# Transformer block on one core: fillers until a slot's last VectorE sum, a second bank for warming matmuls, LayerNorm 2 ahead of VectorE's exps

## The chip, the cores and the metric

The kernel runs on one core of a Trainium2 chip. The metric is the device time in microseconds (us); lower is better. "ACT" is ScalarE, "DVE" VectorE, "PE" TensorE, "POOL" GpSimd, "SP" SyncE (which issues DMAs).

## The reference

x is 2048 x 640, bf16. The block is attention with 32 heads of 20 channels, then a gated MLP of width 1728, each behind a LayerNorm without weights and each added to its input:

```python
qkv = layernorm(x) @ wqkv                       # 32 heads, Dh = 20
p   = softmax(q @ k.T * 20 ** -0.5)             # 2048 x 2048 per head
h   = x + (p @ v) @ wo
out = h + (gelu(layernorm(h) @ w_gate) * (layernorm(h) @ w_up)) @ w_down
```

The first LayerNorm is LN1 here, the second LN2. The softmax is 32 x 2048 x 2048 = 134 million exps, and they are most of the work outside TensorE.

## The kernel before, in words

**A planner writes the order.** The program first collects operations (`op`: engine, instructions, an estimated duration, a priority, what is read and written, PSUM banks taken and given back). Then `Sched.schedule` plays them through in planned time: whenever an engine is free it takes, of the operations that are ready and whose banks are free, the one with the lowest priority number (and on PE prefers the one that keeps the array's mode). The order so found is what each engine's queue gets; `emit` adds the semaphore waits. So a priority or a planned duration has no instruction of its own, but it can change the order on every engine.

**Attention.** The 2048 queries are cut into seven chunks (512, 512, 256, 256, 256, 128, 128). A chunk is worked off in slots (32 in all, 8 for each large chunk, 4 for each of 256, 2 for each of 128); a slot fills one PSUM bank, bank 6, with 4 heads' outputs side by side for 512 columns. Within a slot PE makes tiles of scores (128 keys x 512 columns; line 942, "S"), two or three PSUM banks at a time; ScalarE makes `exp` of them into the buffers `pts`/`pts2` (18 tiles of 512, in turn); PE sums them times V into bank 6 (`pv_op`, tag "O"). A part of the score tiles ("SD", single tiles) goes to VectorE instead: `d_exp` copies the tile out of PSUM (line 877) and makes the exponential in six passes over 1024 or 2048 columns; the sums of these tiles (tag "OD") follow later, at the latest before the slot is closed. When all sums of a slot are done, `epilogue` copies bank 6 out to `osb` (VectorE, line 1025), which frees the bank for the next slot, transposes it (line 1035) and divides by the row sums into `o_nat`. ScalarE can run ahead of the sums only as far as the 18 buffers reach.

**Background.** PE's and VectorE's spare time goes to the other work, in the banks that attention leaves: 7 and 5, and in slots 8 to 15 (chunk 1, where scores use six banks) bank 7 alone (`BG`). In chunk 0 these are the projections. After a chunk's last slot `post` collects the rest of the block for that chunk: `o_nat` is transposed (by DMA on SP's queue for chunks 1 to 5), multiplied with `wo` (line 659), added to x (line 1081); LN2 takes its statistics on VectorE (`ln_stats`: two `bn_stats` of 320 columns and one `bn_aggr` for a tile of 128 tokens), 1/sqrt in 14 small operations on POOL for two tiles together (`ln_rsqrt`), a reciprocal and `ln_apply` on VectorE, DMA transposes; then gate matmuls (line 1114) and copies (line 1149), gelu on ScalarE over all copies of the chunk together, up matmuls (1114 as well) with products (1160), down matmuls (1171) with the last add (1175), and the output's DMA. The last chunk ("tail") has nothing to hide behind: its `post` starts after the last exp.

**Priorities** (a lower number goes first): scores and their copies 0, sums 1, copies that give a bank back 1.8 (`sc.ev`), VectorE's exp passes, epilogue transposes and the tail 2 (`P_EPI`), LN2's matmuls 2.5 (`P_LNP`), LN2 on VectorE and POOL 2.5 (`P_LND`), other background 3.

**Fillers.** PE's clock is granted by use, so the planner adds matmuls without a result. A *zero matmul* group is four matmuls (128 x 32 weights of zeros, 512 columns) that add 0 to bank 6; this is possible while a slot's sums are open in that bank (`live`). They are added to a sum operation, or stand alone where PE has nothing to do. A *warming matmul* writes into a free background bank, bank 7 alone. Both are put in only where PE's planned use over the last 3.4 us is too low:

```python
199                 if e == "pe" and self.pad is not None and o.tag and o.tag[0] == "O":
...
204                     while u < PAD_MIN * PAD_WIN and o.util < 1.1 and o.dur + 0.215 < room:
205                         o.fns = o.fns + self.pad
...
209                     live = o.i not in self.final
```

`final` holds each slot's last sum of ScalarE's exps, so `live` ends there even when sums of VectorE's exps are still to come.

Of the kernel before, what the change touches and what calls it, by code (L numbers as in the profile page):

```python
# [7 lines left out]
ALU = mybir.AluOpType  # L8
# [38 lines left out]
class Sched:  # L47
# [3 lines left out]
    def __init__(self, nc):  # L51
        self.nc = nc
        self.ops = []
        self.lw = {}
        self.rd = {}
        self.warm = None
        self.pad = None
        self.final = set()
        self.ev = 9
# [34 lines left out]
    def schedule(self):  # L94
# [23 lines left out]
        while done < total:  # L118
# [4 lines left out]
            for e in ENGINES:  # L123
# [51 lines left out]
                if chosen is None:  # L175
                    if e == "pe" and self.warm is not None:
                        while recent and recent[0][0] < t - WARM_WIN:
                            recent.popleft()
                        b = self.warm_bank
                        free7 = (owner[b] is None and free_at[b] <= t + 1e-9  # L180
                                 and all(hasattr(ops[d], "fin") and ops[d].fin + 0.06 <= t for d in self.warm_deps))
                        if sum(x for _, x in recent) < WARM_MIN * WARM_WIN and (free7 or live):
                            o = Op()
                            o.i, o.eng, o.lat = len(ops), "pe", DRAIN["pe"]
                            o.prio, o.sem, o.tag, o.util = (9, 0), None, "warm", 0.213
                            o.acq, o.rel, o.succ, o.dur = [], [], [], 0.215
                            if live and (mode[e] == "col" or not free7):
                                o.fns, o.mode, o.deps = list(self.pad), "col", set()
                            else:
                                o.fns, o.mode = [self.warm], "full"  # L190
                                o.deps = set(self.warm_deps) | ({last[b]} if last[b] is not None else set())
                                last[b] = o.i
                            ops.append(o)
                            chosen = o
                            total += 1
                    if chosen is None:
                        continue
                o = chosen
# [128 lines left out]
PV_QUADS = 2  # L327
D_LAG = 9
PR, PR2 = 12, 6
D_QUADS = (1,) + (2,) * 15 + (2, 2) + (3, 2) * 5 + (2, 2, 2, 2)  # L330
# [6 lines left out]
P_QK, P_PV, P_PRO, P_EPI, P_LN, P_BG = 0, 1, 1.5, 2, 2.5, 3  # L337
P_LND, P_LNP = 2.5, 2.5


def bass_sequential_preLN__mha_block__glu_gated_geglu__prompt_kernel(
# [12 lines left out]
    with ExitStack() as es:  # L354
# [545 lines left out]
        def pv_op(s_, quads, acq, seq, after, key):  # L900
# [4 lines left out]
            for have in quads:  # L905
                for kk in range(nk):
                    for pt, pkey, (_, g, kb, j) in have:
# [5 lines left out]
                        pv_open.add((s_, j))  # L913
                        reads += [pkey, ("v", kt, g // 4)]
            return op("pe", fns, 0.222 * len(quads), P_PV, mode="col", util=0.213 * len(quads), reads=reads, writes=[key] + seq,
                      acq=acq, after=after)

        def unit(u):
# [57 lines left out]
            while pv_wait:  # L976
# [74 lines left out]
        def prefetch(c):  # L1051
            q0, nq = CHUNKS[c]
            nt = nq // 128
            tb = base(c)
            op("sp", I("dma_start", h_sb[:, tb:tb + nt, :], x_hbm[q0:q0 + nq, :].rearrange("(t p) d -> p t d", p=128)), 0.08, P_EPI,
               writes=[("h", tb + tt, hf) for tt in range(nt) for hf in range(2)], sem=f"xr{c}", lat=2.0 + nq * 0.0034,
               after=tuple(e_ops) + tuple(w_readers) if c == 0 else ())

        def post(c, first_banks, banks, tail):
# [61 lines left out]
            def cols(k):  # L1121
                return min(512, (NF - k * fn_) * nq)
# [19 lines left out]
            else:  # L1142

                cp, gl = [], []
                for k in range(nb):
# [4 lines left out]
                                 reads=[kg], writes=hkeys(k), rel=[bg], after=first))  # L1150
                for ks in [list(range(i, min(i + 4, nb))) for i in range(0, nb, 4)]:
                    w = 512 * (ks[-1] - ks[0]) + cols(ks[-1])
                    fv = hv(ks[0], w)
                    gl.append(op("act", I("activation", fv, fv, ACT.Gelu_apprx_tanh), c_act(w) + 0.04, -1, mode="gelu",
                                 reads=sum(map(hkeys, ks), []), writes=sum(map(hkeys, ks), []), after=cp))
                for k in range(nb):
                    w = cols(k)
                    fv = hv(k, w)
                    bu, ku = mms(k, wu, "wu", (sc.lw[hkeys(k)[-1]],))
                    hdone.append(op("dve", lambda eng, bu=bu, fv=fv, w=w: eng.tensor_tensor(fv, fv, bank(bu, w),  # L1160
                                                                                                 ALU.mult),
                                    c_dve(w), p, reads=[ku] + hkeys(k), writes=hkeys(k), rel=[bu]))
# [103 lines left out]
```

## Time and profile before

| | |
|---|---|
| time, median of 3 runs | 920.41 us (920.27 to 920.45) |
| profiled execution | 921.39 us, its span 919.4 us |
| granted TensorE clock, mean | 0.991 |
| busy ACT / PE / DVE / POOL | 881.1 / 839.5 / 796.2 / 45.6 us |
| first exp, last exp end | 32.25, 885.04 us |
| ScalarE's table loads | 16, 20.5 us |
| zero matmuls, warming matmuls | 668, 53 |

The profile is one execution seen by the hardware profiler. "Busy" is the time in which an engine runs instructions; for PE, whose matmuls overlap, it is not its peak. A row of the timeline gives start, length, engine, line, operation, out<-in with shapes, and how many of them were merged; in brackets stands the idle time of the engine before it and who ended it. Most instructions have line 362, that of the helper that makes them, and are told apart by tiles: `pts` or `rege` written by ACT are exps, `qt_all` and `rege` on DVE mostly exp passes (their buffers lie in regions named so), `ps<-pts,v_all`, `ps<-rege,v_all` and `ps<-qt_all,v_all` the sums on PE (`rege` holds six of ScalarE's buffers as well as some of VectorE's), `ps<-kt_all,zer` the zero matmuls, `ps<-kt_all` the warming ones.

### The profile page before, as it was taken

What the parts mean: (1) busy time and instruction counts of PE and PEld (TensorE: products, weight loads), DVE (VectorE), ACT (ScalarE), POOL (GpSimd) and SP (SyncE); (2) the same over time, 40 slices, a digit from 0 to 9 for tenths busy, and PEclk for the clock granted to TensorE, in tenths of its full rate; (3) what the DMA queues carried; (4) which work ended last, traced back from release to release, by engine and by line L of the source; (5) the groups of instructions that cost most, each with busy time, mean ns of one, the idle gap of its engine ahead of it and who ended that gap; (6) DMA issues with size and microseconds to landing.
All of it is one profiled execution on the core that took longest, in us unless ns stands there. A gap on an engine that the chain in (4) does not pass through costs nothing.

```text
span 919.4 us, 23006 instructions
## 1 busy us (share of the span) xinstructions
PE 839.5 (91%) x10099; PEld 356.2 (39%) x10099; DVE 796.2 (87%) x1458; ACT 881.1 (96%) x789; POOL 45.6 (5%) x149
## 2 busy tenths in 40 slices
PE   3999999999888987989898999999999899899998
PEld 2432223222232222223342333344444445566677
DVE  8869899999799986887988998989999998959943
ACT  8999899999999999999999999999999999999981
POOL 5000000000002000000011000000201000000200
PEclk9999999999999999999999999999999999999999
DMA  7311021335501000000121000000010001002000
GB/s 258 92 22 43 13 61 35 91 89 137 217 1 30 1 1 1 1 1 16 43 30 31 2 1 1 4 20 24 23 37 2 16 9 39 2 17 39 10 9 23
DMA packets 39515, 34.35 MB, mean 37 GB/s; under 512 B 19436, under 2 KB 36936, under 8 KB 39416
## 3 DMA queue, kind: packets, MB, share of 16 engines
q1 hardware_dynamic: 39416, 32.89, 12.9%
q8 instruction: 79, 1.29, 0.6%
q14 instruction: 20, 0.16, 0.1%
HBM read 20.12 MB, written 8.09 MB: 31 GB/s over the span
## 4 chain that ended last, share of the span: by engine, by line
ACT 67%; PE 23%; DVE 8%; issue 1%; POOL 1%; DMA 0%; DVEq 0%
ACT pts L362 42%; ACT rege L362 23%; PE ps L942 6%; PE ps L1114 5%; PE ps L362 4%; PE ps L659 4%; DVE qt_all L362 3%; PE ps L1171 3%; DVE qt_all L877 1%; DVE rege L877 1%; ACT L362 1%; DVE rege L1149 1%; PE ps L1035 1%; DMA rege<-o_nat 0%; PE ps L601 0%
## 5 line engine op out<-in xcount | busy, mean ns | idle before, releaser
L362 ACT ACTIVATE pts<-ps 128x1024 bf16<-128x1024 f32 (+1 forms) x470 | 563.4, 1358 | 3.8 <-PE ps L942 2.6
L942 PE MATMUL ps<-qt_all,kt_all 32*128 32x256 bf16 (+2 forms) x3584 | 310.1, 290 | 42.9 <-ACT pts L362 23.2
L362 ACT ACTIVATE rege<-ps 128x1024 bf16<-128x1024 f32 (+1 forms) x233 | 289.8, 1353 | 6.1 <-PE ps L362 3.5
L942 PEld LDWEIGHTS ps<-qt_all,kt_all 32*128 32x128 bf16 x3584 | 102.2, 92 | 272.1 <-ACT pts L362 142.4
L362 DVE TENSOR_TENSOR qt_all<-qt_all 128x2048 f16<-128x2048 f16 (+3 forms) x186 | 175.0, 941 | 2.1
L1114 PE MATMUL ps<-rege,regw 128*128 128x256 bf16 (+2 forms) x980 | 159.5, 291 | 12.4 <-ACT rege L362 3.7
L362 PE MATMUL ps<-pts,v_all 128*21 128x256 bf16 (+2 forms) x2070 | 126.6, 293 | 0.0
L877 DVE TENSOR_SCALAR qt_all<-ps 128x512 int16<-128x512 f32 x128 | 87.5, 684 | 16.8 <-PE ps L942 15.5
L877 DVE TENSOR_SCALAR rege<-ps 128x512 int16<-128x512 f32 x128 | 87.6, 685 | 14.7 <-PE ps L942 13.4
L1114 PEld LDWEIGHTS ps<-rege,regw 128*128 128x128 bf16 x980 | 72.6, 98 | 70.9 <-issue 27.0
L362 PE MATMUL ps<-rege,v_all 128*21 128x256 bf16 (+2 forms) x1214 | 93.6, 298 | 0.2
L659 PE MATMUL ps<-regw 128*128 128x512 bf16 (+1 forms) x360 | 87.5, 352 | 2.6 <-ACT regw L607 1.5
L362 DVE TENSOR_SCALAR qt_all<-qt_all 128x1024 f16<-128x1024 int16 (+2 forms) x153 | 84.5, 560 | 1.7
L1171 PE MATMUL ps<-regw,rege 128*128 128x320 bf16 x448 | 77.8, 301 | 1.1 <-DVE rege L1139 0.5
L362 DVE TENSOR_TENSOR rege<-rege 128x1024 f16<-128x1024 f16 (+1 forms) x90 | 61.4, 682 | 0.8
L362 PE MATMUL ps<-kt_all,zer 128*32 128x512 bf16 x668 | 59.8, 398 | 0.0
L362 PEld LDWEIGHTS ps<-pts,v_all 128*21 128x21 bf16 x2070 | 45.4, 91 | 33.8 <-issue 30.4
L1160 DVE TENSOR_TENSOR rege<-rege,ps 128x512 bf16<-128x512 bf16 (+1 forms) x53 | 35.8, 677 | 22.7 <-PE ps L1114 22.3
L362 DVE TENSOR_SCALAR rege<-rege 128x1024 int16<-128x1024 int16 (+2 forms) x115 | 49.3, 442 | 1.0
L1171 PEld LDWEIGHTS ps<-regw,rege 128*128 128x128 bf16 x448 | 37.5, 97 | 32.4 <-issue 16.0
L659 PEld LDWEIGHTS ps<-regw 128*128 128x128 bf16 x360 | 28.8, 99 | 45.0 <-issue 24.2
L1149 DVE CAST rege<-ps 128x512 bf16<-128x512 f32 (+1 forms) x53 | 35.8, 679 | 4.7 <-PE ps L1114 4.7
(105 smaller groups left out, 583.2 us busy)
## 6 DMA issues: line engine op xcount, KB each, us to landing
rege<-in_A_x_dram SPq DMA_DIRECT2D x6, 640.0 KB, 5.1
q_rows<-regw SPq DMA_DIRECT2D x20, 128.0 KB, 1.7
out_dram<-rege SPq DMA_DIRECT2D x16, 160.0 KB, 1.8
regw<-in_B_w_gate_dram SPq DMA_DIRECT2D x1, 2160.0 KB, 11.5
regw<-in_B_w_up_dram SPq DMA_DIRECT2D x1, 2160.0 KB, 16.5
regw<-in_B_w_down_dram SPq DMA_DIRECT2D x1, 2080.0 KB, 21.6
kt_all<-k_rows SPq DMA_DIRECT2D x12, 160.0 KB
qt_all<-q_rows SPq DMA_DIRECT2D x12, 160.0 KB
```

Of the source, the lines that this page charges most:

```text
L362: return lambda eng: getattr(eng, method)(*args, **kwargs)
L659: yield op("pe", lambda eng, l=l, r=r, k=k: eng.matmul(bank(bk, n), l, r, start=(k == 0), stop=(k == len(steps) - 1)), c_mm(n) + cold, pri ...
L877: d_ops.append(op("dve", lambda eng: eng.tensor_scalar(v[:, 512 * h:512 * h + 512], bank(b), EXP_MUL, -32000.0, ALU.mult, ALU.max), c_dve( ...
L942: return lambda eng: eng.matmul(out()[:, kk * nq:(kk + 1) * nq], kt_all[32 * j:32 * j + 32, g, kt * 128:(kt + 1) * 128], qt_all[32 * j:32 ...
L1035: op("pe", lambda eng, tt=tt: eng.transpose(bank(b2)[:, tt * 128:(tt + 1) * 128], osb[:, s, tt * 128:(tt + 1) * 128], identf[:]), c_mm(128 ...
L1114: op("pe", lambda eng, a=a, f=f, fi=fi: eng.matmul(bank(bk)[:, fi * nq:(fi + 1) * nq], w[:, a, F0[f]:F0[f] + 128], hnT[:, a, 128 * tb:128 ...
L1149: cp.append(op("dve", lambda eng, bg=bg, fv=fv, w=w: eng.tensor_copy(fv, bank(bg, w)), c_dve(w), p, reads=[kg], writes=hkeys(k), rel=[bg], ...
L1160: hdone.append(op("dve", lambda eng, bu=bu, fv=fv, w=w: eng.tensor_tensor(fv, fv, bank(bu, w), ALU.mult), c_dve(w), p, reads=[ku] + hkeys( ...
L1171: op("pe", lambda eng, f=f, o=o, hf=hf, bk=bk: eng.matmul(bank(bk, 320), ha_f[:, o:o + 128], wd[:, f, hf * 320:(hf + 1) * 320], start=(f = ...
```

## The change

Five edits:

1. `left` counts a slot's sum operations, O and OD; `live` stays on until the last of them has been issued. An OD operation may now carry zero matmuls too, unless it is the last; the last O operation still may.
2. A warming matmul goes into the first free bank of the current slot's background banks: 7, then 5; in slots 8 to 15 only 7.
3. `P_LND` goes from 2.5 to 1.9: LN2's statistics, POOL chain, reciprocal and apply come ahead of the exp passes (2) and behind the copies that free a bank (1.8).
4. A single score tile for VectorE is planned at 0.21 us also where PE has been idle for over 0.06 us before it.
5. Gate, gelu, up and down of `post` are put in functions, so that chunks named in `MERGE` could share one gelu; `MERGE` is empty.

```diff
-        self.final = set()
+        self.left = {}
...
-                        b = self.warm_bank
-                        free7 = (owner[b] is None and free_at[b] <= t + 1e-9
-                                 and all(hasattr(ops[d], "fin") and ops[d].fin + 0.06 <= t for d in self.warm_deps))
+                        b = next((b for b in self.spare if owner[b] is None and free_at[b] <= t + 1e-9), None)
+                        free7 = b is not None and all(hasattr(ops[d], "fin") and ops[d].fin + 0.06 <= t for d in self.warm_deps)
...
-                                o.fns, o.mode = [self.warm], "full"
+                                o.fns, o.mode = [self.warm[b]], "full"
...
-                if e == "pe" and self.pad is not None and o.tag and o.tag[0] == "O":
+                if e == "pe" and o.tag and o.tag[0] == "S":
+                    self.spare = self.spares[o.tag[1]]
+                if e == "pe" and self.pad is not None and o.tag and o.tag[0] in ("O", "OD"):
+                    s_ = o.tag[1] if o.tag[0] == "O" else o.tag[1][0]
+                    self.left[s_] -= 1
+                    live = self.left[s_] > 0
...
-                    while u < PAD_MIN * PAD_WIN and o.util < 1.1 and o.dur + 0.215 < room:
+                    while u < PAD_MIN * PAD_WIN and o.util < 1.1 and o.dur + 0.215 < room and (live or o.tag[0] == "O"):
...
-                    live = o.i not in self.final
...
-                    if o.tag and o.tag[0] == "SD" and mode[e] != "row":
+                    if o.tag and o.tag[0] == "SD" and (mode[e] != "row" or t - free[e] > 0.06):
                         o.dur = SD_ALONE
...
+MERGE = ()
...
-P_LND, P_LNP = 2.5, 2.5
+P_LND, P_LNP = 1.9, 2.5
...
+            sc.left[s_] = sc.left.get(s_, 0) + 1
             return op("pe", fns, 0.222 * len(quads), P_PV, mode="col", ...
...
-                    sc.final.add(pv)
...
+                gated.append((cp, gelu, ups, lambda: down(c, first, banks, hkeys, hdone)))
+                if c in MERGE:
+                    return
+                for x in gated:
+                    x[1](sum((y[0] for y in gated), []))
+                for x in gated:
+                    x[2]()
+                    x[3]()
+                gated.clear()
+                return
+            down(c, first, banks, hkeys, hdone)
...
-        sc.warm = I("matmul", PS[:, 512 * 7:512 * 8], kt_all[:, 0, 0:128], kt_all[:, 0, 0:512], start=True, stop=True,
-                    skip_group_check=True)
+        sc.warm = {b: I("matmul", PS[:, 512 * b:512 * (b + 1)], kt_all[:, 0, 0:128], kt_all[:, 0, 0:512], start=True, stop=True,
+                        skip_group_check=True) for b in (7, 5)}
+        sc.spare = (7,)
...
-        sc.warm_bank = 7
+        sc.spares = [BG[x[0][0]] for x in units]
```

More of the change, by code (lines that the diff above doesn't have):

```diff
@@ L1057, in prefetch @@
                after=tuple(e_ops) + tuple(w_readers) if c == 0 else ())
+        gated = []
         def post(c, first_banks, banks, tail):
@@ L1142, in post @@
             else:
-                cp, gl = [], []
+                cp = []
                 for k in range(nb):
@@ L1150, in post @@
                                  reads=[kg], writes=hkeys(k), rel=[bg], after=first))
[L1151 to L1162, printed above, removed]
+                def gelu(after):
+                    for ks in [list(range(i, min(i + 4, nb))) for i in range(0, nb, 4)]:
+                        w = 512 * (ks[-1] - ks[0]) + cols(ks[-1])
+                        fv = hv(ks[0], w)
+                        op("act", I("activation", fv, fv, ACT.Gelu_apprx_tanh), c_act(w) + 0.04, -1, mode="gelu",
+                           reads=sum(map(hkeys, ks), []), writes=sum(map(hkeys, ks), []), after=after)
@@ new lines, in ups @@
+                def ups():
+                    for k in range(nb):
+                        w = cols(k)
+                        fv = hv(k, w)
+                        bu, ku = mms(k, wu, "wu", (sc.lw[hkeys(k)[-1]],))
+                        hdone.append(op("dve", lambda eng, bu=bu, fv=fv, w=w: eng.tensor_tensor(fv, fv, bank(bu, w),
+                                                                                                     ALU.mult),
+                                        c_dve(w), p, reads=[ku] + hkeys(k), writes=hkeys(k), rel=[bu]))
@@ new lines, in post, with down @@
+                gated.append((cp, gelu, ups, lambda: down(c, first, banks, hkeys, hdone)))
[9 more added lines that the diff above has]
+            down(c, first, banks, hkeys, hdone)
+        def down(c, first, banks, hkeys, hdone):
+            p = P_BG
+            q0, nq = CHUNKS[c]
+            nt = nq // 128
+            tb = base(c)
+            hb = 1792 * tb
+            fn_ = 512 // nq
```

## The prediction

> **What bounds the kernel now.** I read the page's busy table first, then three stretches of the span, then the stretches at half clock, then single stages.
>
> ```profile
> span 919.4 us, 23006 instructions
> PE 839.5 (91%) x10099; PEld 356.2 (39%) x10099; DVE 796.2 (87%) x1458; ACT 881.1 (96%) x789; POOL 45.6 (5%) x149
> ...
> 0.00:32.25 32.25, 17.80 (x138) 10.64 (x138) 27.83 (x82) 27.51 (x48) 12.85 (x36) 1.00 0.59 200
> 32.25:885.04 852.79, 790.83 (x9584) 320.35 (x9580) 754.19 (x1344) 842.68 (x728) 32.77 (x113) 0.99 0.12 32
> 885.04:919.40 34.36, 30.88 (x386) 25.16 (x382) 14.16 (x34) 10.91 (x14) 0.00 (x0) 1.00 0.06 21
> ```
>
> The columns after the length are busy PE, PEld, DVE, ACT, POOL, then the granted clock. From the first exp to the last (32.25 to 885.04) ScalarE is busy 842.68 of 852.79 us. The change removes no exp, gelu or table load, so at most the 10.1 us of ScalarE's waits can go there. After the last exp PE is busy 30.88 of 34.36 us: the end is PE's, and work done before 885 shortens it. The profiled execution took 921.39 us, of which 919.4 is the span; the median of the three timed runs is 920.41, so I subtract from 921.39 and take off 0.98 for the median.
>
> Where do ScalarE's waits lie? Mostly in five stretches of 3.41 us at half clock.
>
> ```profile
> 88.21:91.62 3.41, 2.02 (x16) 0.69 (x13) 3.41 (x9) 3.41 (x4) 0.00 (x0) 1.00 0.31 95
> 91.62:95.03 3.41, 3.41 (x23) 0.69 (x20) 3.41 (x8) 0.82 (x2) 0.00 (x0) 0.50 0.12 40
> 293.01:296.42 3.41, 2.17 (x28) 0.83 (x23) 3.29 (x9) 3.41 (x4) 0.00 (x0) 1.00 0.26 53
> 296.42:299.83 3.41, 3.41 (x28) 0.79 (x20) 2.96 (x5) 2.57 (x3) 0.00 (x0) 0.50 0.00 0
> 480.74:484.15 3.41, 2.05 (x27) 0.91 (x31) 3.41 (x10) 3.41 (x4) 2.24 (x9) 1.00 0.00 0
> 484.15:487.57 3.42, 3.42 (x44) 1.11 (x44) 2.34 (x6) 2.83 (x3) 1.95 (x8) 0.50 0.25 52
> ...
> 617.27:620.69 3.42, 3.42 (x36) 1.35 (x35) 2.95 (x4) 2.63 (x3) 0.00 (x0) 0.50 0.00 0
> ...
> 668.47:671.89 3.42, 3.42 (x34) 1.79 (x30) 2.65 (x6) 2.29 (x3) 0.00 (x0) 0.50 0.51 149
> ```
>
> ScalarE idles 2.59, 0.84, 0.59, 0.79 and 1.13 us in the five, 5.9 of the 10.1. The stretch ahead of each of the first three has PE busy 2.02 to 2.17 us of 3.41, against 790.83/852.79 = 93% over the whole phase. So the clock halves after a stretch in which PE is little used, though no stretch is empty.
>
> **The change part by part.** *Zero matmuls until the last VectorE sum.* A slot is one pass over a 512-column sum bank (bank 6). The first half-clock stretch stands at slot 1's end:
>
> ```profile
> 87.32 0.61 PE L362 MATMUL ps<-pts,v_all 128*21 128x512 bf16 x7
> ...
> 89.16 1.30 PE L942 MATMUL ps<-qt_all,kt_all 32*128 32x512 bf16 x6 [0.91 <-ACT pts L362]
> ...
> 91.90 0.61 PE L362 MATMUL ps<-rege,v_all 128*21 128x512 bf16 x4
> 92.56 0.69 DVE L362 COPY osb<-ps 128x512 f32<-128x512 f32 x1
> 94.87 2.36 ACT L362 ACTIVATE rege<-ps 128x1536 bf16<-128x1536 f32 x2 [2.59 <-PE ps L362]
> L362 PE MATMUL ps<-kt_all,zer 128*32 128x512 bf16 x668 | 59.8, 398 | 0.0
> ```
>
> The slot's last sum of ScalarE's exps is issued at 87.32, that of VectorE's exps (rege) at 91.90, and between them PE idles 0.91 us with zero matmuls forbidden. The change allows them there: about two groups of four at 0.40 us each. 2.02 us of use becomes some 2.8, so I count this stretch as saved. Its worth is not 2.59: the late sum holds bank 6 anyway until the copy of 92.56 ends at 93.25. Only PE's own steps from 91.90 to 94.87 are lengthened by the clock, some 1.6 us of them on the path (the sum at 91.90 with 0.61, the next slot's first sums with the rest up to 94.87 after 93.25); at full clock about half of that stays, so I take 0.8 us. Bounds: 0 and 2.59. The zeros hide in PE's idle time; without that cover a group would delay the next score matmuls by up to 0.40.
>
> *Warming matmuls into bank 5 as well.* Outside slots 8 to 15 bank 5 is a background bank. It helps where bank 7 is held and PE idles, as ahead of the third stretch:
>
> ```profile
> 483.79 0.39 PE L942 MATMUL ps<-qt_all,kt_all 32*128 32x256 bf16 x6 [0.81 <-ACT pts L362]
> ```
>
> There bank 7 holds the slot's transposed sums. Two or three warming matmuls fit in 0.81 us if bank 5 is free; I count 0.59 us saved, bounds 0 and 0.59.
>
> *LN2 in front of VectorE's exps* (priority 2.5 to 1.9; exps 2.0, bank-releasing copies stay 1.8). Fifteen of the sixteen token tiles go this way. First chunk 0:
>
> ```profile
> 269.42 0.48 DVE L1081 TENSOR_TENSOR rege<-ps,rege 128x320 bf16<-128x320 f32 x1
> ...
> 281.09 0.20 DVE L362 BATCH_NORM_AGGREGATE mv<-stats 128x2 f32<-128x12 f32 x1
> ...
> 291.50 0.44 DVE L362 TENSOR_SCALAR xn_t<-rege,mu,rs 128x640 bf16<-128x640 bf16 x1
> ...
> 298.80 1.03 PE L1114 MATMUL ps<-rege,regw 128*128 128x512 bf16 x2
> ```
>
> The last residual add ends at 269.9, the last statistics 11.4 us later, behind exps. Moved up, the gates start some 10 to 15 us before 298.80 and fill PE in 293 to 296: that stretch's 0.84 us I count as saved. Then chunk 1, from which on the background work is one queue:
>
> ```profile
> 479.24 0.49 DVE L1081 TENSOR_TENSOR rege<-ps,rege 128x320 bf16<-128x320 f32 x1
> ...
> 481.76 0.20 DVE L362 BATCH_NORM_AGGREGATE mv<-stats 128x2 f32<-128x12 f32 x1
> 482.02 0.32 POOL L362 CAST mv<-mv 128x4 bf16<-128x4 f32 x1 [0.70 <-DVE mv L362]
> ...
> 486.50 0.20 POOL L362 TENSOR_TENSOR sd<-nw,rs 128x2 bf16<-128x2 f32 x1
> 488.84 0.16 DVE L362 RECIPROCAL rs<-sd 128x2 f32<-128x2 bf16 x1
> ...
> 493.60 0.44 DVE L362 TENSOR_SCALAR xn_t<-rege,mu,rs 128x640 bf16<-128x640 bf16 x1
> ...
> 497.92 0.81 PE L1114 MATMUL ps<-rege,regw 128*128 128x512 bf16 x3
> ```
>
> The adds end at 479.73. Two statistics and an aggregate (1.1 us) bring 480.9, POOL's chain of 4.7 us 485.6, reciprocal and two applies 486.7 in place of 494.04. From the last apply to the first gate pass 3.9 us of DMA transposes on SP's queue, which keep their order. So 7.3 us at best; copies that keep their place before LN2 (about two of 0.7 us) leave 5.5 to 6; I take 5.5. What is that worth at the end?
>
> ```profile
> L1114 PE MATMUL ps<-rege,regw 128*128 128x256 bf16 (+1 forms) x201 | 23.0, 256 | 0.7 <-DVE rege L1149 0.5
> ...
> L1171 PE MATMUL ps<-regw,rege 128*128 128x320 bf16 x44 | 7.7, 301 | 0.0
> ...
> L1171 PE MATMUL ps<-regw,rege 128*128 128x320 bf16 x112 | 16.2, 299 | 0.6 <-DVE rege L1139 0.5
> L1114 PE MATMUL ps<-rege,regw 128*128 128x128 bf16 x218 | 12.8, 219 | 0.0
> ```
>
> The upper two rows are the groups of 820 to 885.04, the lower two those after it. Of 112 down matmuls after 885 only 28 belong to the last chunk, of 218 gate and up matmuls 140: 84 x 0.145 + 78 x 0.059 = 16.8 us are left over from chunks 4 and 5. From 820 on the background advances (23.0 + 7.7)/65.04 = 0.47 us of PE work per us. A queue that is 5.5 us ahead leaves 2.6 us less behind; bounds 0 (the lead is eaten by bank waits) and 7.3 x 0.47 = 3.4.
>
> The price: what waits behind LN2 on VectorE are the exps' passes, then their sums on PE, the copy that frees bank 6, the next slot's sums, and through the buffers of P ScalarE. Slot 24 ends right after chunk 3's adds:
>
> ```profile
> 689.45 0.49 DVE L1081 TENSOR_TENSOR rege<-ps,rege 128x320 bf16<-128x320 f32 x1
> 690.60 0.40 PE L362 MATMUL ps<-pts,v_all 128*21 128x256 bf16 x8
> ...
> 693.39 0.68 DVE L362 COPY osb<-ps 128x512 f32<-128x512 f32 x1
> ...
> 694.62 0.50 PE L362 MATMUL ps<-pts,v_all 128*21 128x256 bf16 x9
> ...
> L362 DVE BATCH_NORM_STATS2 stats<-rege 128x6 f32<-128x320 bf16 x56 | 25.1, 474 | 0.5 <-DMA rege<-in_A_x_dram 0.5
> ```
>
> Four statistics and two aggregates (4 x 0.474 + 2 x 0.20 = 2.3 us) now go before that copy. At slot 1 ScalarE stopped at 92.28, 4.35 us after the last ScalarE sum ended (87.93). The same distance here is 695.35, while the next sums would run at 696.9 to 697.4: a stall of up to 2.1 us where there is none. Bounds 0 and 2.1; I take 1.0.
>
> *The rest.* The empty merge list leaves the order of gate, gelu, up and down as it is: 0. The longer planned time of a lone score tile adds no instruction; it can only swap neighbours in the order, and one swap can win or lose a half-clock stretch, plus or minus 0.8. I also expect one new half-clock stretch at 0.8, since chunk 0's background ends earlier and leaves PE emptier before 465.
>
> Sum: -2.6 (end), -0.8 -0.59 -0.84 + 0.8 = -1.4 (clock), +1.0 (stall): -3.0. 921.39 becomes 918.4, the median 917.4.
>
> [...]
>
> **The rivals.** *The stall decides.* LN2's passes make the sums late at the ends of slots inside LN2, the next slot's sums wait for bank 6, ScalarE stops. It decides once a slot's copy comes more than about 4 us after its last ScalarE sum and the background's lead is lost to bank waits. For it: VectorE has no gap before 693.39 and slot 1 shows the whole path. Against it: in the other chunks' LN2 the copies come soon after the sum. One stall gives 922.5, two 924.6.
>
> *The lead is eaten.* Background copies, score tiles and epilogues share banks 5 and 7; if these bound the queue, the end keeps its 16.8 us: -1.4 + 1.0, 920.0.
>
> [...]
>
> *All half-clock stretches go.* 0.8 + 0.84 + 0.59 + 0.79 + 1.13 = 4.15 us and the end's 2.6: 913.7.
>
> **How the numbers follow.** Forecast 917.4, chance 0.40 (own range 914.5 to 918.5); all stretches gone 0.08; lead eaten 0.14; fillers idle 0.08; stall 0.30, which is high because the order is planned anew and nothing in it protects a slot's end. 0.2% is 1.84 us, about what a measurement of this kernel can tell from no change. Faster 0.48, same 0.14 + 0.08 = 0.22, slower 0.30. The range takes in the case without half clocks and one stall: 913.5 to 923.0.
>
> **What would show it.** Right: zero matmuls between a slot's last ScalarE sum and its copy near 90; chunk 1's first gate near 492; fewer than 84 left-over down matmuls after the last exp; fewer half-clock stretches. Wrong: ScalarE waiting for sums (PE ps L362) around LN2; as much left over after the last exp; new half-clock stretches at slot ends.

## The result and the profile after

The changed kernel took 915.69 us (median of six runs, 914.24 to 916.19), the kernel before beside it on the same chip 920.34: ratio 0.9946, 95% interval 0.9934 to 0.9959. Forecast were 917.4 us and 913.5 to 923.0. The profiled execution took 916.19 us.

The page's span and busy row of after, and the table by stage: up to the first exp, to the last exp, and the end. The columns are those explained in the prediction.

```profile
span 914.2 us, 22759 instructions
PE 824.1 (90%) x9952; PEld 351.2 (38%) x10017; DVE 794.1 (87%) x1458; ACT 881.1 (96%) x789; POOL 48.2 (5%) x149
...
0.00:33.29 33.29, 18.62 (x136) 10.80 (x138) 27.94 (x82) 27.47 (x48) 12.87 (x36) 1.00 0.57 193
33.29:881.61 848.32, 777.49 (x9439) 317.39 (x9501) 752.96 (x1345) 842.65 (x727) 35.28 (x113) 1.00 0.12 32
881.61:914.20 32.59, 27.98 (x381) 22.97 (x379) 13.18 (x32) 11.02 (x14) 0.00 (x0) 1.00 0.05 16
```

ScalarE's work between the first and the last exp is unchanged (842.65 against 842.68 us), but the stage is 848.32 us long and not 852.79: its waits went from 10.1 to 5.7 us. The end went from 34.36 to 32.59 us. The head is 1.04 us longer; over the profiles of this study it lies anywhere between 32.3 and 33.8 us, also for kernels with the same fillers, and I count it to no edit. -4.47 - 1.77 + 1.04 = -5.2 us, the difference of the spans.

Where did the waits go? Four stretches of the clock's length and the group of the zero matmuls in after:

```profile
88.21:91.62 3.41, 2.83 (x36) 0.84 (x37) 3.41 (x8) 3.41 (x4) 0.00 (x0) 1.00 0.15 53
91.62:95.03 3.41, 3.36 (x35) 0.97 (x27) 3.38 (x8) 2.31 (x3) 0.00 (x0) 1.00 0.31 92
806.97:810.38 3.41, 2.04 (x69) 1.31 (x66) 2.41 (x3) 3.41 (x4) 0.00 (x0) 1.00 0.24 48
810.38:813.80 3.42, 3.42 (x63) 1.82 (x51) 0.00 (x0) 2.44 (x3) 0.00 (x0) 0.50 0.02 5
L366 PE MATMUL ps<-kt_all,zer 128*32 128x512 bf16 x560 | 46.9, 384 | 0.0
```

The place of the first half clock before, 91.62 to 95.03, now runs at 1.00, after a stretch with PE busy 2.83 us and not 2.02; the forecast had been some 2.8. Of five half-clock stretches one is left, at 810.38, and in front of it PE is again busy for only 2.04 of 3.41 us. This is had with fewer zero matmuls, 560 for 668.

The end of slot 1 in the timeline of after:

```profile
88.25 0.61 PE L366 MATMUL ps<-pts,v_all 128*21 128x512 bf16 x7
...
89.12 0.40 PE L366 MATMUL ps<-kt_all,zer 128*32 128x512 bf16 x4
...
90.41 0.40 PE L366 MATMUL ps<-kt_all,zer 128*32 128x512 bf16 x4
...
91.32 0.62 PE L366 MATMUL ps<-kt_all,zer 128*32 128x512 bf16 x8
...
91.77 0.39 PE L366 MATMUL ps<-rege,v_all 128*21 128x512 bf16 x4
...
92.53 0.69 DVE L366 COPY osb<-ps 128x512 f32<-128x512 f32 x1
...
94.31 2.37 ACT L366 ACTIVATE rege<-ps 128x1536 bf16<-128x1536 f32 x2 [1.10 <-PE ps L366]
```

After the last sum of ScalarE's exps (88.25) sixteen zero matmuls stand in PE's gaps, where none was allowed. ScalarE waits 1.10 us and not 2.59, but not all of this is the clock. The head is 1.04 us longer in after, so times are best taken from the last sum of ScalarE's exps: the sum of VectorE's exps comes 3.52 us behind it (91.77), where it came 4.58 us behind it before (87.32 and 91.90). The run a5_dropnew of the next section has the order of after without the new fillers, and separates the two parts:

```profile
87.84 0.61 PE L389 MATMUL ps<-pts,v_all 128*21 128x512 bf16 x7
...
91.19 0.40 PE L389 MATMUL ps<-rege,v_all 128*21 128x512 bf16 x4 [0.21 <-DVE rege L389]
...
94.55 2.37 ACT L389 ACTIVATE rege<-ps 128x1536 bf16<-128x1536 f32 x2 [1.75 <-PE ps L389]
...
98.34 2.52 ACT L389 ACTIVATE pts<-ps 128x1536 bf16<-128x1536 f32 x2 [1.42 <-PE ps L970]
```

There the sum of VectorE's exps comes 3.35 us behind and ScalarE waits 1.75 us. So 0.84 of the 1.49 us belong to the order and 0.65 to the fillers, with which PE's steps run at full clock (1.00 from 91.62 to 95.03). In a5 the half clock lasts for two stretches (92.85 to 99.68), and in the second ScalarE waits another 1.42 us; after has no such wait there.

Chunk 1's LN2 and its first gate:

```profile
476.54 0.48 DVE L1087 TENSOR_TENSOR rege<-ps,rege 128x320 bf16<-128x320 f32 x1
...
483.29 0.17 DVE L366 RECIPROCAL rs<-sd 128x2 f32<-128x2 bf16 x1 [0.32 <-POOL sd L366]
...
484.92 0.43 DVE L366 TENSOR_SCALAR xn_t<-rege,mu,rs 128x640 bf16<-128x640 bf16 x1
...
488.62 0.81 PE L1120 MATMUL ps<-rege,regw 128*128 128x512 bf16 x3 [0.16 <-issue]
```

VectorE now waits 0.32 us for POOL's chain in front of the reciprocal, where the reciprocal stood 2.1 us behind that chain, and the first gate is 9.3 us earlier (488.62 for 497.92). From the end of the last residual add to this gate 11.6 us pass (477.02 to 488.62) in place of 18.2 (479.73 to 497.92). So 6.6 us of the 9.3 lie in LN2 itself; the other 2.7 are adds that come earlier. In a5 the same add ends at 480.77 and the gate stands at 492.60, so the earlier adds are the fillers' work and LN2's part is the order's. Not all of that part needs the priority: in a7_ln2c0, where chunk 1 has the old one, 13.2 us pass.

The end, as groups and as rows:

```profile
L1120 PE MATMUL ps<-rege,regw 128*128 128x128 bf16 x260 | 15.5, 219 | 0.1
...
L1200 PE MATMUL ps<-regw,rege 128*128 128x320 bf16 x58 | 8.6, 299 | 1.0 <-DVE rege L1169 0.5 <-DVE rege L1145 0.5
```

```profile
887.45 1.24 PE L366 MATMUL ps<-kt_all 128*128 128x512 bf16 x5
...
890.03 0.49 DVE L1087 TENSOR_TENSOR rege<-ps,rege 128x320 bf16<-128x320 f32 x1 [2.92 <-PE ps L663]
...
898.96 7.99 PE L1120 MATMUL ps<-rege,regw 128*128 128x128 bf16 x140
```

Without the last chunk's own 28 and 140, there are 30 downs and 120 gates and ups left over, in place of 84 and 78: 30 x 0.145 + 120 x 0.059 = 11.4 us of PE work, not 16.8. That is 5.4 us less, but the end is only 1.77 us shorter. The chain of work that ended last is nearly all PE in the end of before; in after it runs from 883.99 to 894.58 over the last chunk's own steps (the copy of bank 6, transposes, division, residual add, LN2's statistics), VectorE's copies and products of the left-over work, and warming matmuls.

### The profile page after: what moved, and what is told of

It reads as the page before. It is cut to its first block, busy times and chain, and to the rows that moved or that the text cites. A ratio compares the mean times of both kernels' runs of the same rounds, so it can differ in the third digit from the quotient of the medians.

```text
span 914.2 us, 22759 instructions
## 1 busy us (share of the span) xinstructions
PE 824.1 (90%) x9952; PEld 351.2 (38%) x10017; DVE 794.1 (87%) x1458; ACT 881.1 (96%) x789; POOL 48.2 (5%) x149
## 4 chain that ended last, share of the span: by engine, by line
ACT 57%; PE 23%; DVE 17%; POOL 1%; issue 1%; DMA 0%; DVEq 0%
ACT pts L366 36%; ACT rege L366 19%; PE ps L947 6%; DVE qt_all L366 5%; PE ps L366 4%; PE ps L1120 4%; PE ps L663 4%; PE ps L1200 3%; DVE rege L366 3%; DVE qt_all L881 2%; DVE rege L881 2%; DVE rege L1169 1%; DVE rege L1155 1%; ACT L366 1%; DVE regw L701 1%
## 5 line engine op out<-in xcount | busy, mean ns | idle before, releaser
L1120 PE MATMUL ps<-rege,regw 128*128 128x256 bf16 (+2 forms) x952 | 151.0, 288 | 12.1 <-ACT rege L366 3.5
L663 PE MATMUL ps<-regw 128*128 128x320 bf16 (+1 forms) x340 | 82.5, 353 | 4.2 <-ACT regw L611 1.7
L1200 PE MATMUL ps<-regw,rege 128*128 128x320 bf16 x448 | 80.6, 302 | 2.0 <-DVE rege L1169 1.0
L1200 PEld LDWEIGHTS ps<-regw,rege 128*128 128x128 bf16 x448 | 36.3, 97 | 34.4 <-issue 16.0
L366 PE MATMUL ps<-kt_all,zer 128*32 128x512 bf16 x560 | 46.9, 384 | 0.0
L366 PEld LDWEIGHTS ps<-rege,v_all 128*21 128x21 bf16 x1214 | 31.1, 91 | 22.6 <-issue 12.1
```

The source lines that it names most:

```text
L366: return lambda eng: getattr(eng, method)(*args, **kwargs)
L663: yield op("pe", lambda eng, l=l, r=r, k=k: eng.matmul(bank(bk, n), l, r, start=(k == 0), stop=(k == len(steps) - 1)), c_mm(n) + cold, pri ...
L1120: op("pe", lambda eng, a=a, f=f, fi=fi: eng.matmul(bank(bk)[:, fi * nq:(fi + 1) * nq], w[:, a, F0[f]:F0[f] + 128], hnT[:, a, 128 * tb:128 ...
L1200: op("pe", lambda eng, f=f, o=o, hf=hf, bk=bk: eng.matmul(bank(bk, 320), ha_f[:, o:o + 128], wd[:, f, hf * 320:(hf + 1) * 320], start=(f = ...
```

## The experiments

Three theories were set against each other: that the fillers take away half clocks; that LN2's lead shortens the end; and that what counts is the order the planner finds with several edits together, of which no edit alone has its part. The rivals of the prediction (the stall, the eaten lead, fillers without effect) stand beside them.

Runs of one kernel differ by several us, and most of that is the number of half-clock stretches. From a run's span and mean granted clock it is k = (1 - clock) x span / (0.5 x 3.413 us), since a stretch at half clock shows a grant of 0.50 and lasts 3.413 us (seven on end last 23.89 us in a6); k is known to about half a stretch since the clock is given to 0.001. A straight line through a kernel's runs gives its "floor" (time at k = 0) and the price of a stretch. For the kernel before, over 88 runs on several chips, k goes from 1 to 9 and the time from 917.55 to 927.5 us; the line is 915.85 + 1.22 k. The profiled end and the left-over downs / gates and ups are counted as above.

| kernel | median us (range; runs) | ratio to before, 95% | mean k | floor us, price | end us; left over |
|---|---|---|---|---|---|
| before | 920.83 (917.55 to 927.5; 88) | | 4.4 | 915.85, 1.22 | 34.4; 84/78 |
| after | 915.69 (914.24 to 916.19; 6) | 0.9946 (0.9934 to 0.9959) | 0.7 | 914.43, 1.35 | 32.6; 30/120 |
| a5_dropnew | 918.68 (917.01 to 922.59; 12) | 0.9973 (0.9955 to 0.999) | 5.4 | 913.45, 1.00 | 31.9; 30/120 |
| a6_nofill | 944.81 (940.83 to 947.7; 6) | 1.0259 (1.0233 to 1.0284) | 43.5 | | 31.9; 30/120 |
| e1_left | 919.77 (916.51 to 921.79; 12) | 0.9982 (0.9965 to 1.0) | 3.0 | 916.13, 1.12 | 34.4; 84/78 |
| e2_bank5 | 925.52 (916.5 to 927.23; 12) | 1.0037 (1.0012 to 1.0061) | 5.5 | 916.41, 1.39 | 34.4; 84/78 |
| e12_fill | 919.08 (916.28 to 923.46; 12) | 0.9986 (0.9969 to 1.0004) | 2.9 | 915.38, 1.47 | 34.5; 84/78 |
| e3_ln2 | 923.59 (921.68 to 925.0; 12) | 1.0024 (1.0007 to 1.004) | 4.1 | 920.71, 0.63 | 34.6; 84/73 |
| e4_sd | 919.33 (917.58 to 921.45; 12) | 0.9974 (0.9956 to 0.9992) | 1.8 | 917.70, 0.99 | 38.0; 84/129 |
| e34_ln2_sd | 924.42 (922.77 to 928.38; 12) | 1.0034 (1.0014 to 1.0055) | 4.9 | 919.83, 1.01 | 38.9; 68/120 |
| a4_nosd | 916.03 (914.23 to 917.36; 7) | 0.9932 (0.9905 to 0.9958) | 1.5 | 914.79, 0.57 | 32.3; 28/120 |
| a3_noln2 | 923.02 (920.66 to 927.11; 12) | 1.0018 (0.9998 to 1.0038) | 2.5 | 920.36, 1.20 | 46.2; 84/198 |
| a7_ln2c0 | 924.04 (921.83 to 926.0; 11) | 1.0026 (1.0013 to 1.004) | 3.0 | 918.77, 1.65 | 39.6; 84/118 |
| a8_ln2c15 | 918.82 (916.82 to 920.18; 12) | 0.998 (0.9968 to 0.9993) | 2.6 | 916.02, 1.00 | 35.2; 70/86 |

The ratios compare runs on one chip; the medians of different rows partly come from different chips.

**a5_dropnew: the changed kernel's order without the new fillers.** After the planner is done, the 6 zero groups behind a slot's last ScalarE sum and the 26 warming matmuls in bank 5 are taken out of the list; all else stays in place.

```diff
+        for k, o in enumerate(order):
+            if o.tag == "warm" and o.fns[0] is self.warm[5]:
+                continue
+            # likewise zero groups after the slot's last O operation, alone or carried by an OD operation
+            kept.append(o)
-        self.order = order
+        self.order = order = kept
```

> The changed kernel in its own order, every real operation where it was, with only the fillers that the new rules add left out (6 groups of zero matmuls behind a slot's last ScalarE sum or on a VectorE sum, 26 warming matmuls into bank 5). Theory A (the fillers keep the clock): two to four half-clock stretches come back, one of them near 92 us, and the time rises by 0.8 us for each, to 917 to 919 us. Theory B (the new order keeps the clock, the fillers do nothing): at most one half-clock stretch as in the changed kernel, 915 to 916.5 us.

Measured: 918.68 us, 3.0 more than after, with 5.4 stretches for 0.7. The two medians come from different chips; by their ratios to before the difference is 2.5 us. So 32 small fillers are worth 2.5 to 3 us in an order that is otherwise the same. Two stages and one row of the end of a5:

```profile
32.89:885.51 852.62, 777.29 (x9398) 316.18 (x9459) 753.14 (x1345) 843.09 (x727) 35.27 (x113) 0.99 0.12 32
885.51:917.40 31.89, 26.55 (x374) 22.23 (x371) 13.20 (x32) 11.02 (x14) 0.00 (x0) 1.00 0.05 17
...
893.21 0.49 DVE L1110 TENSOR_TENSOR rege<-ps,rege 128x320 bf16<-128x320 f32 x1 [2.20 <-PE ps L686]
```

The exps' stage is as long as before the change (852.62 us), so in these profiled executions the 4.3 us between it and after's 848.32 belong to the fillers. The end is 31.89 us, 2.5 shorter than before, and this belongs to the order. In the changed kernel it is 0.7 longer than here: from the last exp to the last chunk's first residual add pass 7.70 us here and 8.42 in after, where five warming matmuls (887.45, 1.24 us) stand in front of the `wo` matmuls, on the path of the last chunk.

**a6_nofill: the same order without any filler of the planner.**

```diff
+            if o.eng == "pe":
+                if o.tag == "warm":
+                    carry |= set(o.deps)
+                    continue
+                o.deps, carry = set(o.deps) | carry, set()
+                o.fns = [f for f in o.fns if id(f) not in pad]
+            kept.append(o)
```

> The changed kernel in its own order, with all fillers of the planner left out when the instructions are emitted (219 places: every zero matmul and every warming matmul that the planner put in). No result depends on them. If a half clock follows a stretch of 3.41 us in which PE is used little: many more stretches than the 0.7 of the changed kernel, I expect 8 to 15, at 1.0 to 1.3 us each on a floor of 913.5 to 914.4 us: 922 to 932 us. [...]

Measured: 944.81 us and 43.5 stretches, three times as many as I had expected at the most, and 13 us over the expected range. The slices of the clock on its page, and three windows and a row from it:

```profile
PEclk9999899899597997999687999899999989969899
```

```profile
451.09:454.51 3.42, 1.70 (x18) 0.33 (x17) 3.32 (x7) 3.42 (x4) 0.00 (x0) 1.00 0.67 231
454.51:478.40 23.89, 19.83 (x166) 5.91 (x166) 17.04 (x32) 21.54 (x19) 0.00 (x0) 0.50 0.14 29
...
452.96 0.39 PE L962 MATMUL ps<-qt_all,kt_all 32*128 32x512 bf16 x3 [0.95 <-ACT pts L381]
```

In the stretch from 451.09 PE is busy for 1.70 us and its longest idle time is 0.95 us; the half clock that follows lasts seven stretches on end, 23.89 us. So the rival by which fillers do nothing falls. The work of all the removed fillers is gone, and the kernel is 29 us slower.

**e1_left, e2_bank5, e12_fill: the fillers' edits in the order of before.** e1 has only the count `left`, e2 only the second bank, e12 both, without LN2's priority and without the planned time.

```diff
# e1
-                if e == "pe" and self.pad is not None and o.tag and o.tag[0] == "O":
+                if e == "pe" and self.pad is not None and o.tag and o.tag[0] in ("O", "OD"):
+                    s_ = o.tag[1] if o.tag[0] == "O" else o.tag[1][0]
+                    self.left[s_] -= 1
+                    live = self.left[s_] > 0
# e2
-                        b = self.warm_bank
+                        b = next((b for b in self.spare if owner[b] is None and free_at[b] <= t + 1e-9), None)
# e12: after with
-P_LND, P_LNP = 1.9, 2.5
+P_LND, P_LNP = 2.5, 2.5
-                    if o.tag and o.tag[0] == "SD" and (mode[e] != "row" or t - free[e] > 0.06):
+                    if o.tag and o.tag[0] == "SD" and mode[e] != "row":
```

> The kernel before with the zero matmuls allowed until a slot's last VectorE sum, nothing else. Theory A: the half-clock stretch near 92 us goes, 0.8 to 1.5 us off, 919 to 919.6 us. Theory B: 920 to 921 us, the same number of half-clock stretches.

> The kernel before with warming matmuls into bank 5 as well, nothing else. Theory A: one or two of the half-clock stretches at 484, 617 and 668 us go, 0.6 to 1.9 us off, 918.5 to 919.8 us. Theory B: 920 to 921 us, since slot ends hold both banks.

> The kernel before with both edits of the fillers (zero matmuls until the last VectorE sum, warming matmuls into bank 5), without LN2's priority and without the planned time of lone score tiles. Number of half-clock stretches in a run: (1 - clock) x span / (0.5 x 3.413 us). If the two edits together only remove half-clock stretches (the order of the background stays that of before): the end after the last exp stays near 34.4 us with 84 down matmuls left over, the floor without stretches stays near 916.2 us, the stretches fall from 4.5 to 1 or 2, and the median is 917 to 918 us. If LN2's priority is not needed and the fillers alone make the order good: the end shrinks to 32 to 33 us, and the median is that of the changed kernel, 915 to 916 us. If the two edits don't add up: 919 to 921 us with 4 or more stretches.

Measured: the background does not move in any of the three. Their ends have the same left-over work and the length of before (34.46 us in e12, with PE busy for 30.89).

The floors, 915.4 to 916.4 us, are that of before (915.85). Only k differs: 3.0, 5.5 and 2.9 for 4.4. Both edits together take off 1.5 stretches in the mean, and the interval of e12's ratio still holds 1; the second bank alone does not help at all in this order, and is slower by its interval. I had expected 1 or 2 stretches for e12. In the changed order the new fillers take 5.4 down to 0.7. Where each run of e2 with 1 or 2 stretches took 916.5 to 920.2 us, those with 5 and more took 923.1 to 927.2, so it is the stretches that make it slow, not the added matmuls. Why its count is high is open: nothing in the profiled run, which had two, shows it.

**e3_ln2: LN2's priority alone.**

```diff
-P_LND, P_LNP = 2.5, 2.5
+P_LND, P_LNP = 1.9, 2.5
```

> The kernel before with LN2's priority on VectorE and POOL alone (2.5 to 1.9). Theory A: the end shortens by about 2.6 us and the stretch at 296 us keeps full clock, but the one near 92 stays: 917 to 918 us. Theory B (order does all): 915 to 916.5 us. Rival that LN2 ahead of the exps stalls the slots: 921 us or more, with ScalarE waiting for sums.

Measured: slower, 923.59 us, on a floor near 920.7. ScalarE stands still for 2.02 us at the end of slot 20, after a late copy of bank 6 (595.18):

```profile
489.07 0.80 DVE L362 TENSOR_SCALAR xn_t<-rege,mu,rs 128x640 bf16<-128x640 bf16 x2
...
596.84 1.02 ACT L362 ACTIVATE rege<-ps 128x1024 bf16<-128x1024 f32 x1 [2.02 <-PE ps L362]
...
636.60 0.87 DVE L362 BATCH_NORM_STATS2 stats<-rege 128x6 f32<-128x320 bf16 x2
```

This has the shape of the stall of the prediction's first rival, but not its cause: chunk 1's last LN2 operation on VectorE ends at 489.87 and chunk 2's first begins at 636.60, so none stands in front of this copy. The stall comes with the new order, and why is open. The lead is eaten: chunk 1's first gate comes 4.0 us earlier than before (493.90 for 497.92), and still 84 downs are left over.

The rival's own stall shows in e34_ln2_sd below, which has the same priority, the old fillers and the new planned time. It is at slot 24, the slot that the prediction named:

```profile
688.40 0.40 PE L362 MATMUL ps<-pts,v_all 128*21 128x256 bf16 x8
...
691.67 0.20 DVE L362 BATCH_NORM_AGGREGATE mv<-stats 128x2 f32<-128x12 f32 x1
...
693.51 0.40 PE L362 MATMUL ps<-qt_all,v_all 128*21 128x256 bf16 x8
...
694.23 0.68 DVE L362 COPY osb<-ps 128x512 f32<-128x512 f32 x1
...
695.63 2.37 ACT L362 ACTIVATE pts<-ps 128x1536 bf16<-128x1536 f32 x2 [1.21 <-PE ps L362]
```

Chunk 3's statistics and aggregates run from 687.10 to 691.87 among the exp passes, the sum of VectorE's exps follows 5.1 us behind the last sum of ScalarE's, and ScalarE waits 1.21 us. So with the old fillers both rivals occur; in the changed kernel neither shows.

**e4_sd, e34_ln2_sd, a4_nosd: the planned time of a lone score tile.** e4 is before with this line alone, e34 before with it and with LN2's priority, a4 is after without it.

```diff
-                    if o.tag and o.tag[0] == "SD" and mode[e] != "row":
+                    if o.tag and o.tag[0] == "SD" and (mode[e] != "row" or t - free[e] > 0.06):
```

> The kernel before with the new planned time of a lone score tile alone. As predicted (it only swaps neighbours): floor 915.5 to 917 us against 916.3. Theory C: a lower floor, 914 to 915 us.

> The kernel before with LN2's priority and the new planned time, old fillers. Theory C: floor 914 to 915 us, and the stall of 2.0 us at 595 us of LN2 alone is gone. Theory D: floor about 920 us, the stall is still there. In both: 3 to 6 half-clock stretches a run, 1.1 us each.

> The changed kernel with the old planned time of a lone score tile (the fillers and LN2's priority as changed). So far every run's time follows its number of half-clock stretches, 1.0 to 1.4 us each, from a floor that belongs to the order: 916.3 us for the kernel before, 914.4 for the changed one, 920.7 for LN2's priority alone. Theory C (the planned time of the score tile, which I costed at nothing, is what makes LN2's move pay): the floor here is about 920 us, as with LN2 alone. Theory D (the fillers change the order for the better): the floor is 914 to 915 us as in the changed kernel.

Measured: in the changed kernel the line is worth nothing that can be told (a4 916.03 us; ratio 0.9932 with an interval that holds 0.9946). Alone it makes the end 3.6 us longer, with 51 more gates and ups left over behind exps that end 3.5 us earlier (881.52 for 885.04), and has fewer stretches (1.8); together it comes out 0.3% faster. So it does more than swap neighbours, which is what the prediction took it for. With LN2's priority but the old fillers it makes 924.42 us; the stall near 595 us of e3 is gone there, yet the floor is as high. So LN2's priority is slow without the fillers' edits in the plan, with or without this line, and fast with them.

**a3_noln2, a7_ln2c0, a8_ln2c15: LN2's priority taken out of the changed kernel,** for all chunks, for all but chunk 0, for chunk 0 alone.

```diff
# a3
-P_LND, P_LNP = 1.9, 2.5
+P_LND, P_LNP = 2.5, 2.5
# a7
-            pd = P_EPI if tail else P_LND
+            pd = P_EPI if tail else P_LND if c == 0 else 2.5
# a8
+            pd = P_EPI if tail else P_LND if c else 2.5
```

> The changed kernel with LN2's priority back at 2.5. Theory E (LN2's lead is worth 1.5 to 3 us at the end): floor 916 to 917.5 us, as before. Theory C: LN2 alone costs 4 us, so its absence does no harm: floor at or under 914.5 us.

> The changed kernel with LN2 ahead of VectorE's exps in chunk 0 alone; chunks 1 to 5 have the old priority 2.5. If the lead that counts is that of chunks 1 to 5, whose background is one queue to the end: as without the priority at all, much background is left over after the last exp, the end is over 38 us and the median 919 to 924 us. If the lead of chunk 0 is handed on: the end is 32 to 34 us and the median 915.5 to 917.5 us.

> The complement: the changed kernel with LN2 ahead of VectorE's exps in chunks 1 to 5, and the old priority in chunk 0. If the lead of chunks 1 to 5 counts: the end is 32 to 34 us, and one or two half-clock stretches come back near 296 us; the median is 915.5 to 918 us. If what counts is only how the whole order happens to fall: the end may be of any length, and the floor lies 1 to 6 us above that of the changed kernel, 915.5 to 921 us, without relation to the lead.

Measured: the ends of a3, a7 and a8 are 46.20, 39.60 and 35.20 us long. a3's floor of 920.4 us was foreseen by neither theory. Against after, a7 is 7.9 us longer in its span, of which 7.0 are the end; the lead of chunk 0 alone is not handed on. a8 is 2.5 longer, and its end is 2.6 longer: with the priority in chunks 1 to 5 most of the short end is there, not all. The half clock that a8 was expected to bring back near 296 us did not come (its profiled execution has it at 481.73 and 666.05). (a3 has one gelu fewer before its last exp, so its exps end earlier and the end takes that over; the two stages together are 890.1 us for 880.9.) So with the new fillers in the plan the short end needs LN2's priority, in chunks 1 to 5 above all. That the lead itself does it is not isolated: each of these runs is a new order, e3 has a lead without a shorter end, and e4 lengthens the end by 3.6 us without touching LN2.

What goes with the short end shows in PE's work from 600 to 700 us. Gates and ups, then zero matmuls, of before, of e3 and of after:

```profile
L1114 PE MATMUL ps<-rege,regw 128*128 128x256 bf16 x33 | 6.1, 298 | 0.0
...
L362 PE MATMUL ps<-kt_all,zer 128*32 128x512 bf16 x100 | 8.6, 395 | 0.0
```

```profile
L1114 PE MATMUL ps<-rege,regw 128*128 128x256 bf16 x33 | 4.8, 274 | 0.0
...
L362 PE MATMUL ps<-kt_all,zer 128*32 128x512 bf16 x132 | 11.7, 414 | 0.0
```

```profile
L1120 PE MATMUL ps<-rege,regw 128*128 128x256 bf16 x140 | 19.8, 275 | 0.6 <-DVE rege L1169 0.2 <-DVE qt_all L881 0.2
...
L366 PE MATMUL ps<-kt_all,zer 128*32 128x512 bf16 x36 | 3.2, 385 | 0.0
```

In after PE does 140 gates and ups there (and 89 downs) and has little room for zeros; in before and e3 it does 33 (and 112 and 98 downs) and is filled up with 100 and 132 zeros, and what was not done comes after the last exp. This also says why the fillers' count can fall while the clock improves: 64 of the 108 zeros that after has fewer than before are missing here. Why the planner finds this order only with the fillers' edits and LN2's priority together was not traced further.

## Why the prediction was right, point by point

**The end, -2.6 us.** The direction held, and the size by luck: the order's part is -2.5 (a5), the measured end -1.8. The lead was sized well: LN2's own part of it is 6.6 us for the 5.5 taken, under the bound of 7.3, though a7 has 5.0 of them without the priority there. But the left-over fell by 5.4 us of PE work, not 2.6, and a microsecond less of it is worth only half in the end, because the last chunk's own chain binds there for a part of the time. The two misses cancel. The step "a queue that is 5.5 us ahead leaves 2.6 us less behind" failed twice: it took the rate of the order before for that of a new order, in which e3's lead of 4.0 us leaves all 84 downs behind, and it took the end for a sum of PE's work. The other 0.7 us are the warming matmuls in the end, of which the prediction did not think: they were costed in the exps' stage alone.

**The clock, -1.4 us.** Right in kind and mis-sized. The exps' stage lost 4.47 us, 4.3 of them by the fillers (a5 against after). The term counted three stretches out and one in, from one execution; four went, and the number is not fixed to begin with, since the kernel before has 1 to 9. The worth of the first stretch was sized well: 0.65 us of ScalarE's wait there for the 0.8 taken. What the term left out is that a half clock can last for a second stretch, at 1.42 us more in a5, and that other stretches go as well. The 0.84 us of the stretch at 296 us can't be put down to LN2: the profiled executions of e1, e2 and e12, with LN2's old priority, have full clock there too. The case "all half-clock stretches go", given 0.08 at 913.7, is near what the two runs with none took, 914.24 and 914.63. No run shows what the case "fillers idle", given 0.08, takes for granted: without any filler the kernel has 43.5 half-clock stretches (a6).

**The stall, +1.0 us.** It did not come. In slot 24 of after ScalarE waits 0.40 us, and that for scores:

```profile
691.60 0.40 PE L366 MATMUL ps<-pts,v_all 128*21 128x256 bf16 x8
...
693.13 2.37 ACT L366 ACTIVATE rege<-ps 128x1536 bf16<-128x1536 f32 x2 [0.40 <-PE ps L947]
695.24 0.68 DVE L366 COPY osb<-ps 128x512 f32<-128x512 f32 x1
695.38 4.63 ACT L366 ACTIVATE pts<-ps 128x1536 bf16<-128x1536 f32 x4
```

The copy is 3.24 us behind the end of the last ScalarE sum (692.00), under the 4.35 at which slot 1 stopped. The rival itself is real: e34 has this stall at this slot, 1.21 us for the 1.0 taken. What failed is the step that took the place of chunk 3's adds (689.45) from the order before. In after chunk 3's last aggregate is at 682.46, 9 us ahead of the slot's last ScalarE sum. Which slots LN2 meets depends on the order.

**The rest, 0 plus or minus 0.8.** Too narrow, and the step that failed most: I took the edits as separate terms of a sum. As orders, before with one or two of them has floors of 915.4 to 920.7 us, and only the fillers together with LN2's priority reach 914.4 to 914.8. The merge list is empty and nothing in the runs speaks of it.

By the sum, then: -2.6 became -2.5 + 0.7, -1.4 became -4.5, +1.0 became 0, and the head gave +1.0: -5.3 with rounding, -5.2 us in the profiles, for -3.0. The misses of the clock and the stall (-3.1 and -1.0) outweigh those of the end and the head (+0.8 and +1.0), and that put 915.69 between the forecast and the case without half clocks. The total missed by less than the clock's term alone, and the head's part in that is chance.

## What to carry to other kernels

Where an order is written by a planner, a priority is not a local edit: test it with the other edits that go into the plan, since alone it may lose what it wins in company. Fillers for the clock paid here where PE works in short bursts between another engine's releases (32 of them 2.5 to 3 us, a5 against after), but not on the chain that ends the kernel: five of them cost 0.7 us in the end, and leaving them out there is the next thing to try (it was not run). And before a few us are explained, count the half-clock stretches of each run: between two runs of one kernel they can make more than the change does.

## What the runs showed of the hardware

The clock that PE is granted went with the fillers: the mean of the profiled execution is 0.998 in after and 0.919 in a6, which has the same order and none of them. A half clock can follow a stretch of 3.41 us without any gap of that length: the longest idle time of PE in such a stretch is 0.91 us at 88.21 in before, 0.89 at 806.97 in after and 0.95 at 451.09 in a6. PE was busy for 1.70 to 2.17 us in the stretches ahead of half clocks in the rows above and in the prediction's. But busy time is no sharp rule. The prediction shows the stretch ahead of three of before's five half clocks; these are the other two, and two stretches of after:

```profile
613.86:617.27 3.41, 2.42 (x34) 0.95 (x32) 3.32 (x6) 3.41 (x4) 0.00 (x0) 1.00 0.00 0
665.06:668.47 3.41, 2.96 (x43) 1.22 (x42) 3.32 (x6) 3.41 (x4) 0.00 (x0) 1.00 0.00 0
...
339.34:342.75 3.41, 1.65 (x18) 0.41 (x7) 1.46 (x3) 3.38 (x3) 0.00 (x0) 1.00 0.00 0
342.75:346.16 3.41, 2.63 (x17) 0.94 (x18) 0.69 (x1) 3.41 (x3) 0.00 (x0) 1.00 0.03 5
```

In before PE is busy for 2.42 and 2.96 us and the clock halves; in after it is busy for 1.65 us with an idle gap of 1.95 us behind it, and the clock stays full. (A weight load at 340.75 in this stretch has no matmul record; after's page counts 9952 matmuls for 10017 weight loads. In before, which has a record for each load, the clock also stays full behind the stretch from 354.46 with PE busy for 1.58 us.) Three of after's recorded matmuls there are warming ones, 128*128 in the profile's rows; ahead of its half clock at 810.38 stand 28 scores (32*128), sums (128*21) and one warming matmul. Weighting each matmul's moved columns by these two numbers, over 128 x 128, sorts the stretches better. From the first exp to the last, the traces of before and after have 490 stretches at full clock, and 6 of them are followed by a half clock. All 6 have at most 2656 such columns, where only 5 of the 484 others lie; by busy time they reach 2.96 us, where 124 others lie. The weighting is the author's; that the clock goes by it is not shown, since no run isolates it. Once low, the clock can stay so: seven stretches on end in a6, in which PE is busy 19.83 of 23.89 us.

The number of stretches changes from run to run of one program: in the runs of before k goes from 1 to 9, and the times from 917.55 to 927.5 us, 1.1%. In the profiled executions the first half clock begins 2.9 us (before, 91.62), 0.7 us (a5, 92.85) and 1.5 us (after, 810.38) behind a multiple of 3.413 us from the span's start, with no common value. That this makes k differ between runs of one kernel is not isolated. Half clocks come all through the kernel, in before from 91.62 to 668.47.
